# Routing attention with an ELU MLP: three places where the order of work changes

## The chip, the cores and the metric

The kernel runs on one core of a Trainium2 chip. The metric is device time in microseconds (us) of one execution. A core has five engines that run beside each other, each through its own instructions in order: TensorE (PE, whose weight loads are listed apart as PEld), VectorE (DVE), ScalarE (ACT), GpSimd (POOL) and SyncE (SP), which here only issues DMAs.

## The reference

Two parts follow each other. The first is attention in which a query sees only the keys of its own cluster:

```python
q_assign = argmax(einsum('bhsd,hcd->bhsc', q_n, c_n), axis=-1)
k_assign = argmax(einsum('bhsd,hcd->bhsc', k_n, c_n), axis=-1)
mask = q_assign[:, :, :, None] == k_assign[:, :, None, :]
scores = np.where(mask, 0.125 * (q @ k.T), -1e9)
attn = softmax(scores) @ v
```

q, k and v are (4, 8, 768, 64), with 16 clusters per head; the `_n` are normalised vectors. The second is an MLP on the 3072 tokens of width 512: `h = x @ w_in` (512 x 2048), ELU, and `@ w_out` (2048 x 512). Weights arrive as 64-bit floats, and everything is computed in float32.

## The kernel before

**Blocks.** Work is cut into 48 blocks: 4 batches x 3 thirds of the queries (256 each) x 4 pairs of heads. One loop runs over n, the number of the block, and puts out instructions in the order in which they are written; nothing reorders them. In step n stand, one after the other: `values(n - 1)` (p times v into `o_bank`, row sums into a bank `d`, and a short chain on ACT, DVE and POOL, L599 to L607, that makes `xT`), the loads, `scores(n)` (key tile by key tile, L499, with the exponentials L522 on ACT), the masks, and then a part of the MLP of the third that was finished LAG = 7 blocks earlier.

**PSUM.** There are three pairs of banks (`banks`), which scores, hidden layer and row sums take in turn, and the two banks `o_bank` and `f_bank`. A matmul into a bank waits until its former content was read.

**Clusters.** `similar(b, j, at, size)` multiplies queries (j = 0) or keys (j = 1) with the centroids (L377) and transposes the result on DVE (L384). `assign` takes the largest value in each group of 16, compares, and transposes to `hot`, a one-hot matrix (L396 to L410). In batch 0 the mask is added to the scores by another matmul of `hot` (L511), which needs it in the other half of the partitions as well; ACT copies it there (L413), and `masks` (L474) makes the queries' side `qm`. In later batches `key_numbers` (L425, L428) and `query_numbers` (L438, L446) turn `hot` into cluster numbers, and `keep_same` (L457) compares them and zeroes the p of other clusters, in 12 instructions on DVE per block. `sums` adds the tiles of p (L558 to L560), so that the row sums need fewer matmuls.

**The first block.** Before the loop the queries of batch 0 are transposed on PE, the first pair's keys too, `similar(0, 0)` and `assign(0, 0)` are done in two halves, and the other keys are transposed. `scores(0)` then gets the keys' clusters third by third:

```python
for u in range(NT // 2):
    assign(0, 1, u * QS, QS)
    ...
    exponentials(units[u], u)
    weigh(1)
```

**Weights.** `weigh(n)` puts out n of 34 steps that turn a loaded piece of 64-bit weights into float32: on DVE L272, L275, L278 for the piece of two steps ago and L286, L294 for a new one, on ACT L297 between. They are spread over blocks 0 to 8.

**The MLP.** For each third there are four steps: two hidden steps (`hidden`, 32 matmuls of L622, exponential on ACT at L632, POOL at L633), two more, then the products with `w_out` in a scheme with seven instead of eight matrix products (`outer`: four products, then three). The rest of ELU (`elu`, L639 to L643, on DVE) waits in `lag` and comes with the next call of `finish`. The scheme needs sums of blocks of `w_out`: `sum_weights(half)` makes them, four subtractions for each half, on DVE, in block 8 (LAG + 1), one half after the fourth hidden step and one after `finish`.

**The head of a batch.** The clusters of batch b + 1 are found in the last block of batch b. In the first block of the batch (n = 12, 24, 36) come, after `scores(n)`: `key_numbers`, the first `query_numbers`, `keep_same(n)`, `sums(n)`, and then the third hidden step of an earlier third.

Of the kernel before, what the change touches and what calls it, by code (L numbers as in the profile page):

```python
# [15 lines left out]
Alu = mybir.AluOpType  # L16
# [45 lines left out]
def main_path(ctx, tc, c, q, k, v, centroids, moe_w_in, moe_w_out, out):  # L62
    nc = tc.nc
    B, H, S, D = q.shape
# [4 lines left out]
    HS = S // 2  # L69
# [3 lines left out]
    NPR = H // 2  # L73
    KC = DM // P
    FC = DF // P
# [16 lines left out]
    o_bank = long.tile([P, 512], F32, name="o_bank")  # L92
# [77 lines left out]
    for e in range(2):  # L170
# [5 lines left out]
            op=Alu.add,  # L176
# [27 lines left out]
    for e in range(2):  # L204
# [11 lines left out]
        op=Alu.mult,  # L216
# [90 lines left out]
    def weigh(n):  # L307
        for _ in range(n):
            next(rest, None)
# [7 lines left out]
    def w_parts():  # L317
        e_, f_ = w_out[:, : FC // 2, :QS], w_out[:, : FC // 2, QS:]
        g_, h_ = w_out[:, FC // 2 :, :QS], w_out[:, FC // 2 :, QS:]
        return e_, f_, g_, h_  # L320

    def sum_weights(half):

        of = slice(half * FC // 4, (half + 1) * FC // 4)
        e_, f_, g_, h_ = (x[:, of] for x in w_parts())
        t1, t2, t4 = (w_sum[:, n, of] for n in range(3))
        nc.vector.tensor_tensor(t1, f_, e_, op=Alu.subtract)
        nc.vector.tensor_tensor(f_, h_, f_, op=Alu.subtract)
        nc.vector.tensor_tensor(t2, h_, t1, op=Alu.subtract)
        nc.vector.tensor_tensor(t4, g_, t2, op=Alu.subtract)  # L330

# [34 lines left out]

    def similar(b, j, at, size, ps=None):

        if at == 0:
            sim[b, j] = route.tile([P, S], F32, name="sim", tag="sim", bufs=1)
        if ps is None:
            ps = banks()[:, 0]
        cols = slice(at, at + size)
        for pr in range(NPR):
            nc.tensor.matmul(  # L377
                ps[32 * pr : 32 * pr + 32, :size],
                lhsT=cT[:, 32 * pr : 32 * pr + 32],
                rhs=T[b * NPR + pr, j][:, cols],  # L380
                start=True,
                stop=True,
            )
        return lambda: nc.vector.transpose(sim[b, j][:, cols], ps[:, :size])  # L384

    def assign(b, j, at, size):
        if at == 0:
            hot[b, j] = route.tile(
                [P, 2 if b == 0 else 1, S], BF16, name="hot", tag=f"hot{j}", bufs=1
            )  # L390
        cols = slice(at, at + size)
        n = size // NC
        s = sim[b, j][:, cols].rearrange("p (n c) -> p n c", c=NC)
        top = route.tile([P, HS // NC], F32, name="top", tag="top", bufs=1)[:, :n]
        oh = route.tile([P, HS], BF16, name="oh", tag="oh", bufs=1)[:, :size]
        nc.vector.tensor_reduce(top, s, axis=Axis.X, op=Alu.max)  # L396
        at = counted.setdefault(size, [])
        at.append(len(at) + (0 if size == HS else 4 * B - 2))
        at = at[-1]
        nc.vector.scalar_tensor_tensor(  # L400
            oh.rearrange("p (n c) -> p n c", c=NC),
            s,
            1.0,
            top.unsqueeze(2).to_broadcast([P, n, NC]),
            op0=Alu.mult,
            op1=Alu.is_equal,
            accum_out=count[:, at : at + 1],
        )
        h = hot[b, j]
        nc.vector.transpose(h[:, 0, cols], oh)  # L410
        for e in range(2 if b == 0 else 0):
            at = 64 * e
            nc.scalar.copy(h[64 - at : 128 - at, 1, cols], h[at : at + 64, 0, cols])  # L413

    def side(pr, e):
        return int(pr // 2 != e)
# [74 lines left out]
    def scores(n):  # L491
        b, third, pr = blocks[n]
        i = b * NPR + pr
        cols = ts(third, QS)

        def plain(s, kt):
            for e in range(2):
                rows = slice(64 * e, 64 * e + 64)
                nc.tensor.matmul(  # L499
                    s[:, e, ts(kt % 2, QS)],  # L500
                    lhsT=T[i, 1][rows, ts(kt, P)],
                    rhs=T[i, 0][rows, cols],
                    start=n > 0 or kt % 2 == 0,
                    stop=b > 0,
                    skip_group_check=n == 0,
                )

        def mask(s, kt):
            for e in range(2):
                rows = slice(64 * e, 64 * e + 64)  # L510
                nc.tensor.matmul(  # L511
                    s[:, e, ts(kt % 2, QS)],
                    lhsT=hot[b, 1][rows, side(pr, e), ts(kt, P)],
                    rhs=qm[n][rows],
                    start=False,
                    stop=True,
                    skip_group_check=n == 0,
                )

        def exponentials(s, u):  # L520
            p = pu[n, u] = probs.tile([P, 2, 2 * QS], F32, name="p", tag="p")
            nc.scalar.activation(p, s, Act.Exp, scale=SCALE)  # L522

        if n == 0:

            turn_first = similar(0, 1, 0, QS, o_bank)
            turn_rest = similar(0, 1, QS, 2 * QS, f_bank)
            units = [banks() for _ in range(2)]
            for u in range(2):
                for m in range(2):  # L530
                    plain(units[u], 2 * u + m)
            turn_first()
            for u in range(NT // 2):
                assign(0, 1, u * QS, QS)
                if u == 0:
                    turn_rest()
                if u == 1:
                    units.append(banks())
                    for m in range(2):
                        plain(units[2], 4 + m)  # L540
                for m in range(2):
                    mask(units[u], 2 * u + m)
                exponentials(units[u], u)
                weigh(1)
            return
        for u in range(NT // 2):
            s = banks(place["u"][u])
            for m in range(2):
                plain(s, 2 * u + m)
                if b == 0:  # L550
                    mask(s, 2 * u + m)
            exponentials(s, u)
            if n < LAG + 2:
                weigh(1)
# [52 lines left out]
        nc.gpsimd.tensor_tensor(x, x, r, op=Alu.mult)  # L607


    lag = []  # L610

    def finish():
        for step in lag:
# [3 lines left out]
    def hidden(b, third, n):  # L617
        h = banks(place["h"][n % 2])
        hf = h.rearrange("p a (f s) -> p (a f) s", f=2)
        for ch in range(KC):  # L620
            for f in range(4):
                nc.tensor.matmul(  # L622
                    hf[:, f],
                    lhsT=w_in[:, ch, ts(4 * n + f, P)],
                    rhs=xT[b, third][:, ch],
                    start=(ch == 0 and f % 2 == 0),
                    stop=(ch == KC - 1),
                    skip_group_check=True,
                )
        t = g[:, 4 * n : 4 * n + 4]  # L630

        nc.scalar.activation(t, hf, Act.Exp)  # L632
        nc.gpsimd.tensor_scalar(t, t, 1.0, 0.0, op0=Alu.min, op1=Alu.max)  # L633
        finish()
        lag.append(lambda: elu(n, t, hf))
# [147 lines left out]
    for pr in range(NPR):  # L783
        turn(pr, 0)
    turn(0, 1)
    for half in range(2):
        similar(0, 0, half * HS, HS)()
    for pr in range(1, NPR):
        turn(pr, 1)
    for half in range(2):  # L790
        assign(0, 0, half * HS, HS)
    masks(0)

    at_tile = turn_of
    for n in range(len(blocks) + LAG):
# [40 lines left out]
        if n < len(blocks):  # L836
            late = [lambda n=n: sums(n)] if n > LAG else []
            if b > 0:
                third = at // NPR
                q_in = lambda b, third, places: (lambda: query_numbers(b, third, places))  # L840
                if at == 0:
                    key_numbers(b)
                    query_numbers(b, third, [(0, o_bank)])
                    extra[0] = [q_in(b, third, [(1, f_bank), (2, o_bank)])]
                    extra[1] = [q_in(b, third, [(3, f_bank)])]
                elif at % NPR == 0:
                    query_numbers(b, third, [(0, f_bank), (1, o_bank)])
                    extra[0] = [q_in(b, third, [(2, f_bank), (3, o_bank)])]
                keep_same(n)
            if b > 0 and at % NPR == 2:  # L850
                extra[1] = late
            elif not ahead or at + 1 < NB:
                late and late[0]()
# [9 lines left out]
        for m, step in enumerate(main):  # L863
            step()
            for other in extra.get(m, []):
                other()
            if n < LAG + 2 and m < 2:
                weigh(2 if n == LAG else 1)
            if n == LAG + 1 and m > 0:
                weigh(100)  # L870
                sum_weights(m - 1)
        if n == len(blocks) + 1:
            findings()
        if n == len(blocks) + 2:
# [255 lines left out]
```

## Time and profile before

| | |
|---|---|
| median of 9 runs | 1007.83 us (1006.49 to 1009.01) |
| the profiled execution | 1009.9 us, span 1008.1 us |
| PE / PEld busy | 983.6 us (98%) / 770.8 us (76%) |
| DVE / ACT / POOL busy | 661.8 us (66%) / 323.1 us (32%) / 129.6 us (13%) |
| mean granted PE clock | 0.995 of full |

The span reaches from the first instruction to the last. Times in views are us from its start; L499 is line 499 of the kernel before. A view of windows gives, for each stretch, its length, the busy time and the instructions of PE, PEld, DVE, ACT and POOL, the granted clock of PE as a share of full speed, the busy share of the DMA engines, and GB/s. A timeline gives start, duration and instruction, and in brackets how long its engine was idle before it and what ended that.

### The profile page before, as it was taken

The numbers are of one execution on the slowest core, as the hardware profiler recorded it, in microseconds if no ns is written. First come the engines' busy times: TensorE is split into PE (matmuls) and PEld (weight loads), VectorE is DVE, ScalarE is ACT, GpSimd is POOL, SyncE is SP. The second block draws the span as 40 slices with busy tenths as digits, with TensorE's granted clock in tenths as the row PEclk, the third lists the DMA queues.
The fourth block names the chain that finished last, engine by engine and source line by source line (L and its number), as shares of the span: only waits on it lengthen the run. The fifth ranks groups of instructions, "written<-read, shape, count | busy, mean of one in ns | idle before, by whom it ended". The sixth has DMA issues, their size and how long they took to land.

```text
span 1008.1 us, 14617 instructions
## 1 busy us (share of the span) xinstructions
PE 983.6 (98%) x5949; PEld 770.8 (76%) x5949; DVE 661.8 (66%) x1190; ACT 323.1 (32%) x576; POOL 129.6 (13%) x143
## 2 busy tenths in 40 slices
PE   6899999999999999999999999999999999999997
PEld 4566777778878877778788788777877887888886
DVE  7999993666656766796567577587666666663131
ACT  6777432332233232232323232133124224221010
POOL 0001110110210210111111111111021021021010
PEclk9999999999999999999999999999999999999999
DMA  9848132000123123100122113110011010000000
GB/s 288 319 152 200 58 63 53 20 21 25 37 47 63 37 48 64 37 17 17 53 47 48 53 34 61 37 32 16 16 38 32 16 38 26 23 21 1 21 1 24
DMA packets 103962, 55.57 MB, mean 55 GB/s; under 512 B 83408, under 2 KB 96720, under 8 KB 103888
## 3 DMA queue, kind: packets, MB, share of 16 engines
q1 hardware_dynamic: 103888, 54.57, 19.7%
q8 instruction: 48, 0.79, 0.3%
q14 instruction: 26, 0.21, 0.1%
HBM read 48.27 MB, written 6.29 MB: 54 GB/s over the span
## 4 chain that ended last, share of the span: by engine, by line
PE 80%; DVE 17%; ACT 1%; issue 1%; DMA 0%; DVEq 0%; ACTq 0%
PE banks L622 29%; PE f_bank L652 15%; PE o_bank L652 12%; PE o_bank L581 10%; PE banks L499 10%; PE banks L570 2%; DVE ex L272 2%; DVE w_out L275 1%; DVE gT L639 1%; DVE w_out L278 1%; DVE w_in L275 1%; DVE ex L294 1%; DVE w_in L278 1%; DVE oh L400 1%; DVE psum L559 1%
## 5 line engine op out<-in xcount | busy, mean ns | idle before, releaser
L622 PE MATMUL banks<-xT,w_in 128*128 128x256 f32 x1536 | 342.5, 383 | 0.2 <-POOL xT L607 0.2
L622 PEld LDWEIGHTS banks<-xT,w_in 128*128 128x128 f32 x1536 | 290.1, 191 | 48.7 <-issue 9.0
L457 DVE SCALAR_TENSOR_TENSOR p<-qc,kc,p 128x256 f32<-128x256 uint8 x432 | 184.4, 500 | 12.1 <-ACT qc L446 11.9
L499 PE MATMUL banks<-qT,kT 64*128 64x256 f32 x1152 | 146.2, 389 | 2.8 <-DVE gT L639 1.9
L581 PE MATMUL o_bank<-p,v_raw 128*64 128x256 f32 x1152 | 142.9, 385 | 2.2 <-ACT p L522 2.1
L639 DVE SCALAR_TENSOR_TENSOR gT<-gT,banks 128x1024 f32<-128x1024 f32 x48 | 58.4, 1216 | 127.8 <-POOL gT L633 127.8
L632 ACT ACTIVATE gT<-banks 128x1024 f32<-128x1024 f32 x48 | 49.1, 1023 | 286.0 <-PE banks L622 286.0
L522 ACT ACTIVATE p<-banks 128x1024 f32<-128x1024 f32 x144 | 139.3, 1036 | 1.2 <-PE banks L511 0.7
L499 PEld LDWEIGHTS banks<-qT,kT 64*128 64x128 f32 x1152 | 101.4, 186 | 40.5 <-issue 17.8
L581 PEld LDWEIGHTS o_bank<-p,v_raw 128*64 128x64 f32 x1152 | 78.3, 137 | 55.5 <-issue 14.5
L633 POOL TENSOR_SCALAR gT<-gT 128x1024 f32<-128x1024 f32 x48 | 53.6, 1117 | 333.4 <-ACT gT L632 333.4
L607 POOL TENSOR_TENSOR xT<-xT,r 128x256 f32<-128x256 f32 x48 | 40.7, 848 | 427.9 <-DVE r L604 377.7
L599 ACT ACTIVATE r<-banks 128x256 f32<-128x256 f32 x48 | 18.4, 383 | 240.8 <-PE banks L570 240.8
L652 PE MATMUL o_bank<-w_out,gT 128*128 128x256 f32 x416 | 95.1, 382 | 0.0
L652 PEld LDWEIGHTS o_bank<-w_out,gT 128*128 128x128 f32 x416 | 78.2, 190 | 13.5 <-issue 3.3
L652 PE MATMUL f_bank<-w_out,gT 128*128 128x256 f32 x352 | 79.6, 379 | 0.0
L603 DVE TENSOR_TENSOR e<-e,r 128x256 f32<-128x256 f32 x48 | 20.3, 422 | 85.3 <-ACT r L602 85.3
L652 PEld LDWEIGHTS f_bank<-w_out,gT 128*128 128x128 f32 x352 | 66.9, 190 | 9.1
L559 DVE TENSOR_TENSOR psum<-psum,p 128x1024 f32<-128x1024 f32 x40 | 52.7, 1317 | 1.6
L652 PE MATMUL f_bank<-w_sum,gT 128*128 128x256 f32 x224 | 50.9, 380 | 1.0 <-DVE o_sb L692 1.0
L558 DVE TENSOR_TENSOR psum<-p 128x1024 f32<-128x1024 f32 x40 | 48.8, 1221 | 0.0
L652 PEld LDWEIGHTS f_bank<-w_sum,gT 128*128 128x128 f32 x224 | 42.3, 190 | 7.8 <-DVE o_sb L692 2.2
(134 smaller groups left out, 820.9 us busy)
## 6 DMA issues: line engine op xcount, KB each, us to landing
v_raw<-in_v_dram SPq DMA_DIRECT2D x48, 384.0 KB, 3.2
w_sum<-in_moe_w_out_dram SPq DMA_DIRECT2D x12, 512.0 KB, 5.1
out_dram<-o_sb SPq DMA_DIRECT2D x24, 256.0 KB, 2.0
q_raw<-in_q_dram SPq DMA_DIRECT2D x48, 96.0 KB, 3.2
k_raw<-in_k_dram SPq DMA_DIRECT2D x48, 96.0 KB, 3.1
w_sum<-in_moe_w_in_dram SPq DMA_DIRECT2D x8, 512.0 KB, 8.3
w_out<-in_moe_w_in_dram SPq DMA_DIRECT2D x8, 512.0 KB, 11.1
w_out<-in_moe_w_out_dram SPq DMA_DIRECT2D x4, 512.0 KB, 3.7
```

Of the source, the lines that this page charges most:

```text
L457: nc.vector.scalar_tensor_tensor(p, qc[b, third][:, 2 * pr + e], kc[b][:, 2 * u + m, 2 * pr + e : 2 * pr + e + 1], p, op0=Alu.is_equal, op ...
L499: nc.tensor.matmul(s[:, e, ts(kt % 2, QS)], lhsT=T[i, 1][rows, ts(kt, P)], rhs=T[i, 0][rows, cols], start=n > 0 or kt % 2 == 0, stop=b > 0 ...
L522: nc.scalar.activation(p, s, Act.Exp, scale=SCALE)
L558: nc.vector.tensor_tensor(to, pu[n, 0], pu[n, 1], op=Alu.add)
L559: nc.vector.tensor_tensor(to, to, pu[n, 2], op=Alu.add)
L581: nc.tensor.matmul(o_bank[64 * e : 64 * e + 64, :QS], lhsT=raw["v", n][:, e, kt], rhs=p[:, e, ts(m, QS)], start=(kt == 0), stop=(kt == NT ...
L607: nc.gpsimd.tensor_tensor(x, x, r, op=Alu.mult)
L622: nc.tensor.matmul(hf[:, f], lhsT=w_in[:, ch, ts(4 * n + f, P)], rhs=xT[b, third][:, ch], start=(ch == 0 and f % 2 == 0), stop=(ch == KC - 1),
L632: nc.scalar.activation(t, hf, Act.Exp)
L633: nc.gpsimd.tensor_scalar(t, t, 1.0, 0.0, op0=Alu.min, op1=Alu.max)
L639: nc.vector.scalar_tensor_tensor(t, t, -1.0, hf, op0=Alu.add, op1=Alu.max)
L652: nc.tensor.matmul(to[:, :QS], lhsT=left[:, f], rhs=right[:, f], start=(f == 0), stop=(f == FC // 2 - 1),)
```

## The change

There are three parts.

1. At the head of a batch, `key_numbers`, the first `query_numbers`, `keep_same` and `sums` are put into a list `between`, which `hidden` works off after the second of its four rounds of matmuls.
2. `sum_weights` becomes a generator: the first two subtractions of a half stand ahead of the last ELU step of that third, those of the other half and the remaining four after it. `sums` of block 9 (LAG + 2) moves behind the second product.
3. Before the first block, only the first half of the queries' clusters is found, and kept in the memory of `g_sum`. The second half's similarity is put out after the second unit of scores, its transpose and `assign` after the third. `assign` copies only one way; the other way is copied for all columns at once in `other_rows`. The first three weight steps come after all that.

```diff
+    def sum_weights():
+
+        halves = [slice(half * FC // 4, (half + 1) * FC // 4) for half in range(2)]
+        for of in halves:
...
+            nc.vector.tensor_tensor(t1, f_, e_, op=Alu.subtract)
+            nc.vector.tensor_tensor(f_, h_, f_, op=Alu.subtract)
+            yield
+        for of in halves:
...
+            nc.vector.tensor_tensor(t2, h_, t1, op=Alu.subtract)
+            nc.vector.tensor_tensor(t4, g_, t2, op=Alu.subtract)
+        yield
...
     def similar(b, j, at, size, ps=None):
 
-        if at == 0:
+        if (b, j) == (0, 0):
+            sim[b, j] = g_sum.rearrange("p f n -> p (f n)")[:, :S]
+        elif at == 0:
             sim[b, j] = route.tile([P, S], F32, name="sim", tag="sim", bufs=1)
...
         nc.vector.transpose(h[:, 0, cols], oh)
-        for e in range(2 if b == 0 else 0):
-            at = 64 * e
-            nc.scalar.copy(h[64 - at : 128 - at, 1, cols], h[at : at + 64, 0, cols])
+        if b == 0:
+            nc.scalar.copy(h[64:, 1, cols], h[:64, 0, cols])
+
+    def other_rows(j):
+
+        nc.scalar.copy(hot[0, j][:64, 1], hot[0, j][64:, 0])
...
                 exponentials(units[u], u)
-                weigh(1)
+                if u == 1:
+                    turn_more = similar(0, 0, HS, HS, f_bank)
+            turn_more()
+            assign(0, 0, HS, HS)
+            for j in range(2):
+                other_rows(j)
+            weigh(3)
             return
...
                     stop=(ch == KC - 1),
                     skip_group_check=True,
                 )
+            if ch == 1:
+                for other in between:
+                    other()
+                between.clear()
...
-    for half in range(2):
-        similar(0, 0, half * HS, HS)()
+    similar(0, 0, 0, HS)()
     for pr in range(1, NPR):
         turn(pr, 1)
-    for half in range(2):
-        assign(0, 0, half * HS, HS)
+    assign(0, 0, 0, HS)
     masks(0)
...
                 if at == 0:
-                    key_numbers(b)
-                    query_numbers(b, third, [(0, o_bank)])
+
+                    between.append(lambda b=b: key_numbers(b))
+                    between.append(q_in(b, third, [(0, o_bank)]))
+                    between.append(lambda n=n: keep_same(n))
+                    between.extend(late)
+                    late = []
...
-            if b > 0 and at % NPR == 2:
+            if b > 0 and at % NPR == 2 or n == LAG + 2:
                 extra[1] = late
...
-            if n == LAG + 1 and m > 0:
+            if n == LAG + 1 and m == 1:
                 weigh(100)
-                sum_weights(m - 1)
+                sums_left = sum_weights()
+                next(sums_left)
+        if n == LAG + 1:
+            for _ in sums_left:
+                pass
```

More of the change, by code (lines that the diff above doesn't have):

```diff
@@ L320, in w_parts @@
         return e_, f_, g_, h_
[L322 to L330, printed above, removed]
+    def sum_weights():
+        halves = [slice(half * FC // 4, (half + 1) * FC // 4) for half in range(2)]
+        for of in halves:
+            e_, f_, g_, h_ = (x[:, of] for x in w_parts())
+            t1, t2, t4 = (w_sum[:, n, of] for n in range(3))
+            nc.vector.tensor_tensor(t1, f_, e_, op=Alu.subtract)
+            nc.vector.tensor_tensor(f_, h_, f_, op=Alu.subtract)
+            yield
+        for of in halves:
+            e_, f_, g_, h_ = (x[:, of] for x in w_parts())
+            t1, t2, t4 = (w_sum[:, n, of] for n in range(3))
+            nc.vector.tensor_tensor(t2, h_, t1, op=Alu.subtract)
+            nc.vector.tensor_tensor(t4, g_, t2, op=Alu.subtract)
+        yield
     T, sim, hot, qm, qc, kc = {}, {}, {}, {}, {}, {}
@@ L607, in values @@
         nc.gpsimd.tensor_tensor(x, x, r, op=Alu.mult)
-    lag = []
+    lag, between = [], []
     def finish():
@@ L841, in main_path @@
                 if at == 0:
-                    key_numbers(b)
-                    query_numbers(b, third, [(0, o_bank)])
+                    between.append(lambda b=b: key_numbers(b))
[3 more added lines that the diff above has]
+                    late = []
                     extra[0] = [q_in(b, third, [(1, f_bank), (2, o_bank)])]
                     extra[1] = [q_in(b, third, [(3, f_bank)])]
[L846 to L849, printed above, removed]
-            if b > 0 and at % NPR == 2:
+                else:
+                    if at % NPR == 0:
+                        query_numbers(b, third, [(0, f_bank), (1, o_bank)])
+                        extra[0] = [q_in(b, third, [(2, f_bank), (3, o_bank)])]
+                    keep_same(n)
+            if b > 0 and at % NPR == 2 or n == LAG + 2:
                 extra[1] = late
```

## The prediction

> **What bounds the kernel now.** I read the page first, then the windows by stage, then the timeline where PE or DVE stands idle. PE is busy 983.6 us of the span of 1008.1, so all gaps of PE together are 24.5 us; 5.3 of them lie before the first matmul and 6.1 after the last, and the change touches neither. What it can win is in the gaps between, and in stretches at a lower clock. The windows (span, then busy us of PE, PEld, DVE, ACT, POOL, then clock):
>
> ```profile
> 14.40:46.80 32.40, 27.37 (x220) 16.56 (x220) 29.73 (x67) 24.38 (x44) 1.03 (x1) 0.95 0.98 372
> 46.80:145.00 98.20, 95.26 (x737) 67.44 (x734) 96.27 (x163) 62.06 (x104) 11.86 (x11) 1.00 0.46 119
> 160.00:200.00 40.00, 40.00 (x268) 29.93 (x264) 20.57 (x34) 11.21 (x19) 4.95 (x6) 1.00 0.10 34
> 200.00:220.00 20.00, 18.37 (x95) 14.65 (x94) 15.44 (x30) 6.84 (x13) 1.76 (x2) 0.91 0.07 21
> 220.00:1000.00 780.00, 778.23 (x4504) 623.42 (x4504) 482.06 (x856) 210.15 (x383) 107.41 (x99) 1.00 0.13 33
> ```
>
> From 160 us on PE is the bound, with holes at the heads of batches. From 14 to 145 us DVE is full (96.27 of 98.20): it rebuilds the weights (steps of L272 to L294) beside everything else, and PE follows it. How DVE's order holds PE in the start is seen in the timeline (start, us, instruction, then in brackets the idle time before it and who ended it):
>
> ```profile
> 18.81 0.41 DVE L384 STREAM_TRANSPOSE sim<-o_bank 128x256 f32<-128x256 f32 x1
> 26.03 0.69 DVE L272 SCALAR_TENSOR_TENSOR ex<-w_sum,ex 128x512 uint32<-128x512 uint32 x1 [0.98 <-ACT ex L297]
> 34.05 0.72 ACT L297 ACTIVATE ex<-ex,off 128x512 uint32<-128x512 uint32 x1 [1.88 <-DVE ex L294]
> 35.45 0.70 PE L499 MATMUL banks<-qT,kT 64*128 64x256 f32 x4 [0.88 <-ACT e L600]
> 38.17 0.99 PE L581 MATMUL o_bank<-p,v_raw 128*64 128x256 f32 x4 [1.36 <-ACT p L522]
> 46.72 0.43 DVE L603 TENSOR_TENSOR e<-e,r 128x256 f32<-128x256 f32 x1 [0.97 <-ACT r L602]
> ```
>
> ACT stands at L297 until DVE gives it the exponents of a weight step; L599 to L602 and the next exponentials queue behind it, and PE waits for those. After 14.4 us DVE itself idles only twice, 0.98 and 0.97 us. The other places that the change touches, on PE:
>
> ```profile
> 139.70 0.70 PE L499 MATMUL banks<-qT,kT 64*128 64x256 f32 x4 [1.42 <-DVE gT L639]
> 152.40 3.72 PE L652 MATMUL f_bank<-w_sum,gT 128*128 128x256 f32 x16 [0.79 <-DVE o_sb L692]
> 204.94 0.23 PE L425 MATMUL f_bank<-index,hot 128*128 128x8 bf16 x3 [1.42 <-DVE hot L410]
> 205.41 8.86 PE L622 MATMUL banks<-xT,w_in 128*128 128x256 f32 x32
> 444.18 0.23 PE L425 MATMUL f_bank<-index,hot 128*128 128x8 bf16 x3 [0.77 <-DVE hot L410]
> 681.53 0.23 PE L425 MATMUL f_bank<-index,hot 128*128 128x8 bf16 x3 [0.78 <-DVE hot L410]
> ```
>
> The same 32 matmuls of L622 take 7.17 us elsewhere. Why they took 8.86 here is in the windows of 1 us (the clock is the third number from the end):
>
> ```profile
> 205.00:206.00 1.00, 1.00 (x7) 0.68 (x8) 0.62 (x3) 0.68 (x2) 0.20 (x1) 0.80 0.00 0
> 206.00:207.00 1.00, 1.00 (x4) 0.81 (x3) 0.86 (x2) 0.11 (x1) 0.53 (x1) 0.50 0.03 8
> 209.00:210.00 1.00, 1.00 (x6) 0.88 (x5) 1.00 (x4) 0.00 (x0) 0.00 (x0) 0.99 0.00 0
> ```
>
> The clock was 0.50 for about 3.4 us after the gap, and PE lost 1.7 us. The waits at 35.45 and 38.17 were followed by the same (0.50 from 38.4 to 41.8); the equal wait at 139.70 was not.
>
> **Heads of batches.** key_numbers, the first query_numbers, keep_same and sums move behind the first 16 matmuls of the first MLP step (half of 7.1 us, so 3.55). The keys' last one-hot is there at 204.9, and PE now comes to it at 203.1 + 3.55 = 206.7: no wait. Removed are 0.21 + 1.42, 0.77 and 0.78, together 3.2 us. The 0.7 us of small matmuls stay. In the profiled execution the clock's 1.7 us go too, since PE now has no gap there.
>
> What the move delays is DVE: qc lands at about 208.1 instead of 206.1, the 12 mask multiplies (5.02) end at 213.1 and the sums (1.22 + 1.23 + 0.69) at 216.2. Queued behind them is L639 of the third hidden step, which ran at 216.49 and now runs at 216.2. PE needs the masked p first in values, after a second hidden step, at 218.9, and the sums 2.7 us later. Cover: 5 us. Without it each head would give back 2 to 3 us. On ACT L428 and the first cast go ahead of L632, which only comes after the hidden step.
>
> **Weights' sums.** Before, all eight subtractions in two groups of four stand in DVE's queue; the first group (132.93 to 138.43) holds L639 of the last hidden step, and PE waits 1.42 us for its bank. After, two of them (1.22 + 1.94) stand ahead: L639 starts at 136.05 and ends at 137.3, while PE asks at 138.3. So 1.42 goes. The other six follow and end at about 145, as now. sums of block 9 (3.15 us, from 147.64) now come after the second product instead of before the first, so L687 and L692 are done at 148.9 and 149.3; PE, now 1.42 earlier, asks for f_bank at 150.1. So 0.79 goes as well. Late next is nothing: row sums of block 9 are at 156, their input at 153.6. Sum: -2.2.
>
> **Start.** It takes 8 matmul passes, one transpose (0.5) and one assign (1.65) of DVE, six copies of ACT (three of 0.51, three of 0.41) and two weight steps (0.63 each) from ahead of, or between, the first masks, and puts them behind the third. What stays in front is bounded elsewhere. kT's last copy on ACT waits for its six PE transposes, which wait for the last k load: issued at 11.8, 4.4 on its way, so 16.2; the copy ends at 18.04, and the first key similarity is ready at 18.75 against 18.81 now. PE's own 16 score passes of L499 end at 21.5 either way.
>
> - PE: masks of unit 0 end at 21.7 (22.3 now), exponentials at 21.8, 23.7, 25.6 (22.30, 24.23, 26.91), values(0) at 25.4 instead of 26.80. PE leads by 1.4 us.
> - DVE: it idles from 16.7 (queries' half done) to 18.75, 2.05 us, where it now does the second half. After the keys it waits 0.6 us for the second half's matmuls, which stand behind unit 1's masks on PE; transpose and assign end at 26.6, two weight steps at 27.9. L272 needs L297, and on ACT that now stands behind the exponentials (to 26.6), one copy of 0.51 and the two of other_rows. Those are 64x768; from the 64x384 (0.51) and 64x256 (0.41) copies I estimate 0.83 each. L297 ends at 29.6, so DVE idles 1.7. Sum 2.05 + 0.6 + 1.7 - 0.98 = 3.4, with 0.2 of lost overlap at the restarts 3.6 us late.
> - DVE is full from here to 145, so this isn't made up, and PE's lead of 1.4 turns into a longer wait at the place of 35.45. One thing gives: the 0.97 us at 46.72, which came from the slow clock. If the clock is back by 41.8, it goes wholly; if the longer wait of PE (about 6 us, 33 to 39) holds it down one stretch more, 0.8 returns. I take +0.4.
>
> Start in the profiled execution: 3.6 - 0.97 + 0.4 = +3.0. Bounds: 2.65 and 4.4; -1.4 if DVE's delay met slack that I can't see.
>
> [...]
>
> **Sum.** Profiled execution: +3.0 - 2.2 - 3.2 - 1.7 = -4.1 against its own time of 1009.9 (span 1008.1 and 1.8 around it), 1005.8. It is 2.1 above the median of 1007.83. The nine runs spread over 2.5 us, and the two clock losses are worth 1.7 + 0.97; I take it that the median has about half of them. Then the heads' clock gives 0.85 and the start costs 3.6 - 0.5 + 0.4 = 3.5: 3.5 - 2.2 - 3.2 - 0.85 = -2.75, so 1005.1 (-0.27%). With start and clock at their bounds, 1003.4 to 1006.8. A measurement of this kernel can tell about 0.2%, 2.0 us, from no change, so this is close to that line.
>
> **Rivals.**
> - Slower: the clock at the start. PE's wait from 33 to 39 is four times that of any now; if the clock stays at 0.50 over three stretches of 3.4 us, PE loses 5.1, with only some 0.3 us of idle time in each block of 9.2 to take it up: 3.6 + 5.1 - 5.4 = +3.3, 1011.1. It decides from 3.6 us of half clock on (3.6 + 1.8 = 5.4). For it: the stretch from 38.4 holds only some 2 us of PE work. Against it: both stretches now end after one. 0.11.
> - No clock loss in the median run, and the start's whole 3.6 + 0.4: 4.0 - 5.4 = -1.4, 1006.4. For it: the median is 2.1 under the profiled run. 0.22.
> - Two groups of sums do as before: the wait at 139.70 returns at f_bank, where the cover is only 0.8 us: 2.2 lost, 1007.3. 0.05.
> - The start costs nothing, or keeps PE's 1.4: -5.4 - 0.85 = 1001.6, or 1000.2. For it: PE's gaps from 23 to 27 do shrink. Against it: DVE's 96.27 of 98.20. 0.10.
> - The forecast: 0.52.
>
> **How the numbers follow.** Faster by over 0.2%: 0.52 + 0.10 = 0.62; within: 0.22 + 0.05 = 0.27; slower: 0.11. The range goes from the last rival's near end, 1001.6, to past the third's 1007.3, 1007.5; left out are the slower case and half of the last, 0.16.
>
> **What would show it.** Right: no PE wait before L425, and 7.1 us of L622 with 0.7 between its halves; L639 ahead of the last six subtractions, no wait at L499 and f_bank; DVE's first L272 at about 29.6 and still full to 145; a PE wait of some 6 us before scores of block 1. Wrong: a first L272 before 27, first key transpose well before 18.7, DVE gaps after 50 us, or a half clock of over 4 us at 40.

## The result and the profile after

The changed kernel takes 1004.25 us in the median of 9 runs (1003.17 to 1005.11), the kernel before 1007.73 (29 runs, 1005.92 to 1009.01): a ratio of 0.9966, 95% interval 0.9958 to 0.9974, so 3.5 us less. The profiled execution takes 1003.53 us, span 1001.8. Lines of the new kernel that answer to those of before: L385 for L377 and L392 for L384 (similarity and its transpose), L510 for L499 (scores), L598 for L581 (values), L639 for L622 (hidden), L660 for L639 (ELU), L673 for L652 (product), L436 for L425 (key numbers), L533 for L522 (exponentials), L424 is `other_rows`, L617, L619, L620 are L600, L602, L603. Windows of the changed kernel, columns as before:

```profile
14.40:46.80 32.40, 24.95 (x205) 14.44 (x203) 27.77 (x62) 22.24 (x35) 1.03 (x1) 0.89 0.95 354
46.80:145.00 98.20, 96.62 (x753) 69.10 (x752) 96.27 (x166) 63.42 (x109) 11.86 (x11) 1.00 0.49 123
200.00:220.00 20.00, 20.00 (x120) 15.77 (x120) 15.44 (x30) 7.55 (x12) 4.50 (x3) 1.00 0.06 19
```

In the first, the start, PE and DVE are both about 2 us less busy than before (27.37 and 29.73), and the clock is 0.89. In the second PE is busy 1.4 us longer, in the third 1.6, the gap at the head; it is full there. DVE's queue in the start (timeline of DVE, instructions with idle time before them), then ACT's beside it:

```profile
17.80 0.45 DVE L392 STREAM_TRANSPOSE sim<-o_bank 128x256 f32<-128x256 f32 x1 [1.71 <-PE o_bank L385]
23.55 0.58 DVE L392 STREAM_TRANSPOSE g_sum<-f_bank 128x384 f32<-128x384 f32 x1 [0.65 <-PE f_bank L385]
28.84 0.69 DVE L272 SCALAR_TENSOR_TENSOR ex<-w_sum,ex 128x512 uint32<-128x512 uint32 x1 [1.58 <-ACT ex L297]
```

```profile
26.50 1.56 ACT L424 COPY hot<-hot 64x768 bf16<-64x768 bf16 x2
28.08 1.33 ACT L297 ACTIVATE ex<-ex,off 128x512 uint32<-128x512 uint32 x2
```

These are the three waits that the prediction listed (2.05, 0.6, 1.7), the last because L297 stands behind the two copies. PE in the timeline, at the start, at the sums, and at the first and second head:

```profile
38.18 1.23 PE L510 MATMUL banks<-qT,kT 64*128 64x256 f32 x4 [5.69 <-ACT e L617]
40.89 1.12 PE L598 MATMUL o_bank<-p,v_raw 128*64 128x256 f32 x4 [0.21 <-ACT p L533]
...
137.52 0.70 PE L510 MATMUL banks<-qT,kT 64*128 64x256 f32 x4
...
140.98 3.72 PE L673 MATMUL o_bank<-w_out,gT 128*128 128x256 f32 x16
...
151.45 3.62 PE L673 MATMUL f_bank<-w_sum,gT 128*128 128x256 f32 x16
...
201.94 3.72 PE L639 MATMUL banks<-xT,w_in 128*128 128x256 f32 x16
205.50 0.29 PE L436 MATMUL f_bank<-index,hot 128*128 128x8 bf16 x6
205.73 0.39 PE L449 MATMUL o_bank<-hot,index 32*128 32x256 bf16 x2
206.04 3.72 PE L639 MATMUL banks<-xT,w_in 128*128 128x256 f32 x16
...
442.01 0.29 PE L436 MATMUL f_bank<-index,hot 128*128 128x8 bf16 x6
```

No line from 137.52 on has a bracket: the waits of 1.42, 0.79, 1.42 and 0.77 are gone, and none has come in their place. The clock, in windows of 1 us:

```profile
36.00:37.00 1.00, 0.00 (x0) 0.00 (x0) 1.00 (x4) 0.23 (x1) 0.00 (x0) 0.50 1.02 397
41.00:42.00 1.00, 1.00 (x6) 0.62 (x8) 0.97 (x2) 1.00 (x2) 0.32 (x1) 0.50 0.96 347
206.00:207.00 1.00, 1.00 (x6) 0.87 (x5) 0.23 (x1) 0.61 (x2) 0.00 (x0) 1.00 0.00 0
```

PE waits 5.69 us, from 32.5 to 38.18. The clock falls to 0.50 inside this wait, at 35.4, and comes back at 42.2, after 6.8 us, twice the 3.4 of either stretch in the trace of before; 2.8 of these 6.8 us lie in the wait and slow nothing. At the head the clock stays full.

Where the profiled execution's time went can be read off at marks that both traces have. Each row is the move of a mark from before to after, less the move of the mark ahead of it:

| mark | before, after (us) | its part | predicted |
|---|---|---|---|
| first transpose of the queries' similarity (L384, L392) | 14.36, 13.71 | -0.65 | 0 |
| first hidden step of the first third | 95.14, 96.82 | start: +2.33 | +3.0 |
| values behind the fourth product | 156.05, 154.99 | sums: -2.74 | -2.2 |
| values behind head 1 | 221.95, 217.44 | -3.45 (1.7 of it clock) | -1.63 - 1.7 |
| values behind head 2 | 459.51, 453.96 | -1.04 | -0.77 |
| values behind head 3 | 696.86, 690.48 | -0.83 | -0.78 |
| sum | | -6.38 | -4.1 |

The first row isn't the change's: over all kernels of this study that mark lies anywhere from 13.7 to 14.4, whichever start they have. The row of head 2 holds one more wait of PE than the prediction listed, in the trace of before:

```profile
393.90 3.72 PE L652 MATMUL f_bank<-w_sum,gT 128*128 128x256 f32 x16 [0.21 <-DVE o_sb L692]
```

The changed kernel's trace has no such wait.

### The profile page after: what moved, and what is told of

It is laid out like the page before. It is cut to its first block, busy times and chain, and to the rows that moved or that the text cites. A ratio compares the mean times of both kernels' runs of the same rounds, so it can differ in the third digit from the quotient of the medians.

```text
span 1001.8 us, 14614 instructions
## 1 busy us (share of the span) xinstructions
PE 979.9 (98%) x5949; PEld 768.5 (77%) x5949; DVE 663.4 (66%) x1190; ACT 322.4 (32%) x573; POOL 133.9 (13%) x143
## 4 chain that ended last, share of the span: by engine, by line
PE 88%; DVE 9%; SPq 1%; ACT 0%; DMA 0%; issue 0%; DVEq 0%
PE banks L639 32%; PE f_bank L673 16%; PE o_bank L673 13%; PE banks L510 11%; PE o_bank L598 11%; DVE ex L272 2%; PE banks L587 2%; DVE w_in L275 1%; DVE w_in L278 1%; DVE w_out L275 1%; DVE ex L294 1%; DVE w_out L278 1%; PE banks L385 1%; SPq L135 1%; PE f_bank L449 1%; DVE w_out L286 1%
## 5 line engine op out<-in xcount | busy, mean ns | idle before, releaser
L639 PE MATMUL banks<-xT,w_in 128*128 128x256 f32 x1536 | 341.6, 382 | 0.3 <-POOL xT L624 0.3
L639 PEld LDWEIGHTS banks<-xT,w_in 128*128 128x128 f32 x1536 | 288.7, 190 | 49.0 <-issue 10.7
L510 PE MATMUL banks<-qT,kT 64*128 64x256 f32 x1152 | 147.2, 390 | 6.2 <-ACT e L617 5.7
L598 PE MATMUL o_bank<-p,v_raw 128*64 128x256 f32 x1152 | 142.5, 385 | 1.1 <-ACT p L533 1.1
L533 ACT ACTIVATE p<-banks 128x1024 f32<-128x1024 f32 x144 | 139.2, 1036 | 2.0 <-PE banks L522 1.7
L510 PEld LDWEIGHTS banks<-qT,kT 64*128 64x128 f32 x1152 | 101.7, 187 | 44.0 <-issue 18.3
L660 DVE SCALAR_TENSOR_TENSOR gT<-gT,banks 128x1024 f32<-128x1024 f32 x48 | 58.4, 1216 | 114.4 <-POOL gT L654 114.4
L598 PEld LDWEIGHTS o_bank<-p,v_raw 128*64 128x64 f32 x1152 | 78.1, 137 | 54.3 <-issue 14.2
L654 POOL TENSOR_SCALAR gT<-gT 128x1024 f32<-128x1024 f32 x48 | 57.9, 1206 | 324.0 <-ACT gT L653 324.0
L673 PE MATMUL o_bank<-w_out,gT 128*128 128x256 f32 x416 | 95.1, 382 | 0.0
L673 PEld LDWEIGHTS o_bank<-w_out,gT 128*128 128x128 f32 x416 | 78.2, 190 | 13.5 <-issue 3.3
L673 PE MATMUL f_bank<-w_out,gT 128*128 128x256 f32 x352 | 79.6, 379 | 0.0
L620 DVE TENSOR_TENSOR e<-e,r 128x256 f32<-128x256 f32 x48 | 20.3, 422 | 84.3 <-ACT r L619 84.3
L673 PEld LDWEIGHTS f_bank<-w_out,gT 128*128 128x128 f32 x352 | 66.9, 190 | 9.1
L576 DVE TENSOR_TENSOR psum<-psum,p 128x1024 f32<-128x1024 f32 x40 | 54.8, 1370 | 1.5
L673 PE MATMUL f_bank<-w_sum,gT 128*128 128x256 f32 x224 | 50.8, 380 | 0.0
L673 PEld LDWEIGHTS f_bank<-w_sum,gT 128*128 128x128 f32 x224 | 42.4, 190 | 6.5 <-DVE o_sb L713 0.8
```

Of the source, the lines that this page charges most:

```text
L510: nc.tensor.matmul(s[:, e, ts(kt % 2, QS)], lhsT=T[i, 1][rows, ts(kt, P)], rhs=T[i, 0][rows, cols], start=n > 0 or kt % 2 == 0, stop=b > 0 ...
L576: nc.vector.tensor_tensor(to, to, pu[n, 2], op=Alu.add)
L598: nc.tensor.matmul(o_bank[64 * e : 64 * e + 64, :QS], lhsT=raw["v", n][:, e, kt], rhs=p[:, e, ts(m, QS)], start=(kt == 0), stop=(kt == NT ...
L639: nc.tensor.matmul(hf[:, f], lhsT=w_in[:, ch, ts(4 * n + f, P)], rhs=xT[b, third][:, ch], start=(ch == 0 and f % 2 == 0), stop=(ch == KC - 1),
L660: nc.vector.scalar_tensor_tensor(t, t, -1.0, hf, op0=Alu.add, op1=Alu.max)
L673: nc.tensor.matmul(to[:, :QS], lhsT=left[:, f], rhs=right[:, f], start=(f == 0), stop=(f == FC // 2 - 1),)
```

## The experiments

**The theory.** The three parts are independent: heads and sums take PE gaps away, and the start costs what it adds to DVE's idle time, because DVE is full up to 145 us. **The rivals.** The start costs through the clock and not through DVE; or ACT's copies and the weight steps cost it and not the queries; or the cover of DVE at the heads is smaller than I took it. The kernels of the experiments have line numbers of their own, so a line is known by its operands.

### Each part alone, and two together

*heads_only*: the kernel before, with part 1 of the change and nothing else.

```diff
                 if at == 0:
-                    key_numbers(b)
-                    query_numbers(b, third, [(0, o_bank)])
+                    between.append(lambda b=b: key_numbers(b))
+                    between.append(q_in(b, third, [(0, o_bank)]))
+                    between.append(lambda n=n: keep_same(n))
...
```

> The kernel before with the first part alone (numbers of a new batch's clusters behind the first half of its first MLP step). Theory: the three gaps of PE ahead of the key numbers go, 1.7, 1.0 and 1.0 us by the shift of the later groups in the two traces, and the half clock after the first of them where a run had it (1.7): -3.7 to -5.4 us, about 1003.2. Rival: the mask multiplies, 2 to 3 us later on VectorE, give it back: -1 us or less, with a wait of PE at the values of that block.

Measured: 1003.09 us, ratio 0.9960 (0.9947 to 0.9973), 4.7 us less.

*sums_only*: the kernel before, with part 2 alone.

```diff
-                sum_weights(m - 1)
+                sums_left = sum_weights()
+                next(sums_left)
+        if n == LAG + 1:
+            for _ in sums_left:
+                pass
```

> The kernel before with the second part alone (subtractions of the weights split around the last ELU, sums of block 9 after the second product). Theory: the waits at 139.7 and 152.4 go, 1.42 + 0.79 us as listed and some 0.5 more by the shift of the later groups: -2.2 to -2.8 us, about 1005.2. Rival: the wait moves on to the fourth product or to the row sums of block 9: within 0.5 us of the kernel before.

Measured: 1004.99 us, ratio 0.9975 (0.9966 to 0.9984), 2.8 us less. Its trace keeps the wait at the head, but not what followed it in the trace of before. PE's timeline and a window of 1 us:

```profile
200.53 0.23 PE L431 MATMUL f_bank<-index,hot 128*128 128x8 bf16 x3 [1.42 <-DVE hot L416]
```

```profile
202.00:203.00 1.00, 1.00 (x6) 0.90 (x5) 1.00 (x3) 0.00 (x0) 0.12 (x1) 1.00 0.02 8
```

The same 1.42 us, and the clock stays at 1.00. So the gap alone doesn't bring the clock's loss at the head; what does was not shown.

*start_only*: the kernel before, with part 3 alone.

```diff
-    for half in range(2):
-        similar(0, 0, half * HS, HS)()
+    similar(0, 0, 0, HS)()
...
-                weigh(1)
+                if u == 1:
+                    turn_more = similar(0, 0, HS, HS, f_bank)
+            turn_more()
+            assign(0, 0, HS, HS)
...
+            weigh(3)
```

> The kernel before with the third part alone (first block given half of the queries' clusters and one copied half of the rows). Theory: VectorE, full from 14 to 145 us, loses about 3.4 us in three waits (2.05, 0.6, 1.6 against 0.98 before) and only 0.97 comes back at the place of 46.7: +2.5 to +3.6 us, about 1010.7, and a wait of PE of over 5 us before the scores of block 1. Rival: PE's lead of 1.4 us at the first values lasts, or the delay of VectorE is absorbed: -1.4 to 0 us.

Measured: 1010.29 us, ratio 1.0029 (1.0018 to 1.0041), 2.5 us more. DVE's three waits are there again (1.50, 0.65 and 1.58). The three parts alone add up to 5.0 us less, the whole change has 3.5. Each of these figures is known to about 1 us either way, so the runs neither show that the parts share something nor that they are quite independent.

*heads_sums*: the changed kernel with part 3 undone, which is the kernel before with parts 1 and 2 (the diff of start_only, backwards).

> The changed kernel with its third part undone (first and second part on the kernel before). Theory: the sum of the first two, -5.9 to -8.2 us, about 1000.7, so some 3 us below the changed kernel's 1004.25. Rival that the start costs nothing or gains: 1004.3 or above. Third reading, that the parts share gaps: less than the sum of the runs with one part each.

Measured: 1000.70 us (999.60 to 1000.99), ratio 0.9931 (0.9918 to 0.9945), 7.1 us less; the sum of the two alone is 7.5. It beats both kernels, and of the versions below only rows_only is level with it: the start takes back half of what the other two parts bring. DVE's idle time from the first transpose of the queries' similarity to 145 us, in its timeline:

```profile
25.47 0.69 DVE L272 SCALAR_TENSOR_TENSOR ex<-w_sum,ex 128x512 uint32<-128x512 uint32 x1 [0.99 <-ACT ex L297]
28.36 0.69 DVE L272 SCALAR_TENSOR_TENSOR ex<-w_sum,ex 128x512 uint32<-128x512 uint32 x1 [0.20 <-ACT ex L297]
```

1.19 us, where the changed kernel has 3.94.

### What in the start costs: copies, weight steps, clock

*after_again*: the changed kernel once more.

> The changed kernel itself, on the chip and in the rounds of the three others: 1003.2 to 1005.1, median about 1004.2.

Measured: 1004.02 us, ratio 0.9960 (0.9946 to 0.9973). In this trace the half clock lies from 38.2 to 45, 2.8 us later than in the first, and DVE waits once more:

```profile
50.00 0.43 DVE L620 TENSOR_TENSOR e<-e,r 128x256 f32<-128x256 f32 x1 [1.05 <-ACT r L619]
```

ACT's r comes from the row sums of values(1), which PE does up to 48 us.

*rows_late*: `other_rows` behind the three weight steps.

```diff
-            for j in range(2):
-                other_rows(j)
             weigh(3)
+            for j in range(2):
+                other_rows(j)
```

> The changed kernel with the two copies of other_rows put behind the first three weight steps instead of ahead of them. Theory: VectorE's wait of 1.58 us at its first L272 is for L297, which stands behind the copies on ScalarE (1.56 us); with them behind it, VectorE waits 0.3 us at most, and since it is full to 145 us the whole kernel is 1.2 to 1.6 us shorter: about 1002.8. Rival: the wait is made by the exponentials and the late second half, or VectorE's delay isn't what the end sees: within 0.4 us of the changed kernel (1004.25).

Measured: 1003.41 us, ratio 0.9953 (0.9940 to 0.9967): 0.6 us under after_again, where I expected 1.2 to 1.6; the two intervals overlap almost wholly, so the medians alone show no gain. DVE's timeline:

```profile
27.62 0.69 DVE L272 SCALAR_TENSOR_TENSOR ex<-w_sum,ex 128x512 uint32<-128x512 uint32 x1 [0.18 <-ACT ex L297]
48.45 0.42 DVE L620 TENSOR_TENSOR e<-e,r 128x256 f32<-128x256 f32 x1 [1.19 <-ACT r L619]
```

The wait at L272 did fall from 1.58 to 0.18, as the theory has it. The trace of after_again has a wait at L620 too (1.05), so against it DVE idles 1.3 us less in all (3.72 against 5.05, table below). The first trace of the changed kernel has none at L620, and against that one (3.94) nearly all of the gain is lost again.

*steps_between*: a weight step after each unit again, as in the kernel before.

```diff
+                weigh(1)
             turn_more()
...
-            weigh(3)
```

> The changed kernel with one weight step after each unit of the first block again, as before the change, instead of three at the end. Theory: two of VectorE's three waits (0.65 for the second half's matmuls, 1.58 at L272) are filled, only the one for the keys (1.7) stays: -1.8 to -2.3 us against the changed kernel, about 1002.2, although the first values begin 1 us or more later on PE. Rival, that PE's early start counts: +0.6 to +1.3 us, about 1005.2.

Measured: 1005.04 us, ratio 0.9972 (0.9959 to 0.9984): 1.0 us over after_again, where I expected about 2 less. My expectation fell. DVE's timeline, then ACT's:

```profile
34.18 0.69 DVE L272 SCALAR_TENSOR_TENSOR ex<-w_sum,ex 128x512 uint32<-128x512 uint32 x1 [1.56 <-ACT ex L297]
50.20 0.42 DVE L620 TENSOR_TENSOR e<-e,r 128x256 f32<-128x256 f32 x1 [1.59 <-ACT r L619]
```

```profile
30.61 1.56 ACT L424 COPY hot<-hot 64x768 bf16<-64x768 bf16 x2
32.18 1.22 ACT L485 ACTIVATE qm<-hot,minus,big 64x256 bf16<-64x256 bf16 x2
33.43 1.33 ACT L297 ACTIVATE ex<-ex,off 128x512 uint32<-128x512 uint32 x2
```

With the steps spread, the copies and L485 come later and stand ahead of another L297. The wait has moved, from 28.84 to 34.18, and kept its size.

*clock_kept*: 24 matmuls more inside PE's wait before the scores of block 1, their results unused.

```diff
+            for _ in range(24 if (n, u) == (1, 2) else 0):
+                nc.tensor.matmul(
+                    f_bank[:, :QS], lhsT=ident, rhs=T[0, 0][:, :QS], start=True, stop=True
+                )
```

> The changed kernel with 24 added matmuls into f_bank, whose result nobody reads, in PE's wait of 5.7 us before the third unit of block 1's scores. Theory: the half clock from 35.4 to 42.2 goes, but costs next to nothing, since PE waits for VectorE and ScalarE there: within 0.4 us of the changed kernel. Rival, the slow clock at the start as a price of its own: -0.8 to -1.7 us.

Measured: 1006.05 us, ratio 0.9983 (0.9974 to 0.9992), 2.0 us over after_again. It didn't do what I meant: PE's timeline has

```profile
32.78 10.63 PE L566 MATMUL f_bank<-qT,ident 128*128 128x256 f32 x48
```

48 records, two for each fp32 matmul, 0.22 us each. PE came to the scores at 43.34 instead of 38.66. The clock stayed at 1.00, but nothing follows from that for its price. What it does tell: PE being 4.7 us late, with the clock full, cost 2.0.

*clock_short*: the same with 10 matmuls.

> The changed kernel with 10 matmuls more (20 passes, about 4.4 us at full clock) into a free bank, inside PE's wait of 5.7 us before the scores of block 1; their results are not used. They should end at about 37.4, before the scores' 38.2. The clock should be 1.00 from 33 to 46 us. Theory (half clock during the first values of block 1 makes ACT's r late, and DVE idles 1 us at L620): that idle time goes, 0.7 to 1.2 us under the changed kernel (about 1003.0). Rival (PE's half clock costs nothing there, since DVE is full anyway, and the idle time at L620 has another cause): within 0.4 us of the changed kernel, and a wait at L620 stays.

Measured: 1003.62 us, ratio 0.9960 (0.9946 to 0.9973), the same ratio as after_again. PE's timeline:

```profile
32.74 4.58 PE L566 MATMUL f_bank<-qT,ident 128*128 128x256 f32 x20
38.50 0.70 PE L510 MATMUL banks<-qT,kT 64*128 64x256 f32 x4 [1.18 <-ACT e L621]
```

This time they fit, the clock is 1.00 from 33 to 46 us, and DVE has no wait at L620. The median moved by 0.4 us, which the measurement can't tell from nothing. So the half clock goes with 1.05 us of DVE's idle time at L620 in one execution (that of after_again) and with none in another (the first trace of the changed kernel, where it ends at 42.2 and L620 doesn't wait); in the median no price of it is seen. The intervals, some 1.3 us either way, don't shut out a small one. But the trace without half clock has the same interval as the first of the changed kernel (83.18 and 83.11 us, table below), so the rival that makes the clock the cause of the start's 3 to 3.5 us falls.

### Which part of the start

*rows_only*: parts 1 and 2, and of part 3 only the copies (one way in `assign`, `other_rows` behind the third masks).

```diff
-        for e in range(2 if b == 0 else 0):
-            at = 64 * e
-            nc.scalar.copy(h[64 - at : 128 - at, 1, cols], h[at : at + 64, 0, cols])
+        if b == 0:
+            nc.scalar.copy(h[64:, 1, cols], h[:64, 0, cols])
...
                 weigh(1)
+            for j in range(2):
+                other_rows(j)
```

> Parts 1 and 2, and of part 3 only the rows: the first block's three early copies of ACT into the other half of hot are left for two larger ones behind its third masks; queries and weight steps as before. Theory (DVE's idle time up to 52 us is what the start costs): DVE's order is untouched, ACT has about 1.3 us less ahead of its first L297, so the wait of 0.99 us at DVE's first L272 shrinks and none of 1.5 us comes in its place; 0.3 to 1.0 us under the kernel with parts 1 and 2 (ratio about 0.9925 to the kernel before). Rival (the two larger copies, 1.56 us on ACT, hold a later L297 as they did in the changed kernel): a wait of 1 to 1.6 us at another L272, 0.5 to 1.5 us over it (ratio about 0.9940).

Measured: 1000.86 us, ratio 0.9931 (0.9917 to 0.9945), the same as heads_sums. Neither forecast came true: DVE's timeline shows both at once,

```profile
25.65 0.69 DVE L272 SCALAR_TENSOR_TENSOR ex<-w_sum,ex 128x512 uint32<-128x512 uint32 x1 [0.66 <-ACT ex L297]
31.76 0.69 DVE L272 SCALAR_TENSOR_TENSOR ex<-w_sum,ex 128x512 uint32<-128x512 uint32 x1 [0.82 <-ACT ex L297]
```

a shorter first wait (0.99 before) and a new one of 0.82 behind the larger copies, 1.48 against 1.19 in all.

*q_only*: parts 1 and 2, and of part 3 only the queries' second half.

```diff
-    for half in range(2):
-        similar(0, 0, half * HS, HS)()
+    similar(0, 0, 0, HS)()
...
+                if u == 1:
+                    turn_more = similar(0, 0, HS, HS, f_bank)
                 weigh(1)
+            turn_more()
+            assign(0, 0, HS, HS)
```

> Parts 1 and 2, and of part 3 only the queries: the second half of the first block's queries is compared and assigned behind its third masks; copies and weight steps as before. Theory: DVE waits about 2.0 us for the keys at 16 to 18 us and 0.6 us for the half moved, and nothing takes the 2 us back, while L297 has no larger copies ahead of it: 2.0 to 2.8 us over the kernel with parts 1 and 2, so about 4.5 us under the kernel before (ratio 0.9955), and with the rows' part this is the whole of the start. Rival (the start's cost is the weight steps and copies around L297, the queries' wait is made up): under 1 us over it (ratio 0.9935).

Measured: 1004.06 us, ratio 0.9965 (0.9952 to 0.9979). That is 3.4 us over heads_sums (0.9965 - 0.9931), more than the 2.0 to 2.8 that I expected, and level with the whole change: the queries' half alone has the start's cost. DVE's timeline:

```profile
18.19 0.45 DVE L392 STREAM_TRANSPOSE sim<-o_bank 128x256 f32<-128x256 f32 x1 [1.50 <-PE o_bank L385]
25.28 0.69 DVE L272 SCALAR_TENSOR_TENSOR ex<-w_sum,ex 128x512 uint32<-128x512 uint32 x1 [0.80 <-ACT ex L297]
33.34 0.69 DVE L272 SCALAR_TENSOR_TENSOR ex<-w_sum,ex 128x512 uint32<-128x512 uint32 x1 [0.51 <-ACT ex L297]
49.38 0.42 DVE L615 TENSOR_TENSOR e<-e,r 128x256 f32<-128x256 f32 x1 [1.61 <-ACT r L614]
```

DVE stands 1.50 us waiting for keys that can't come earlier. The moved half then delays the steps behind it, and with them ACT's L297 and e; PE gets e late (a wait of 2.96 before the scores) and r comes late to DVE (1.61).

**All starts in one table.** Each trace is measured from its first transpose of the queries' similarity to the first hidden step of the first third; DVE's idle time in between (the brackets of its timeline) is taken off. The last column is the median of the runs; all these kernels but the first have parts 1 and 2.

| kernel | interval (us) | DVE idle | rest | median |
|---|---|---|---|---|
| before | 80.78 | 1.95 | 78.83 | 1007.73 |
| heads_sums | 80.00 | 1.19 | 78.81 | 1000.70 |
| rows_only | 80.27 | 1.48 | 78.79 | 1000.86 |
| rows_late | 82.98 | 3.72 | 79.26 | 1003.41 |
| changed kernel | 83.11 | 3.94 | 79.17 | 1004.25 |
| clock_short | 83.18 | 3.99 | 79.19 | 1003.62 |
| q_only | 83.54 | 4.42 | 79.12 | 1004.06 |
| after_again | 84.29 | 5.05 | 79.24 | 1004.02 |
| steps_between | 84.88 | 5.78 | 79.10 | 1005.04 |
| clock_kept | 85.96 | 6.70 | 79.26 | 1006.05 |

The rest is 78.8 with the old order and 79.1 to 79.3 with the queries' half moved; what the 0.3 to 0.5 more are was not shown. So the interval is DVE's work plus what DVE idles, whoever caused it: DVE bounds the start. And the kernel is late by it: against heads_sums the profiled executions from rows_only down to clock_kept are 0.3, 3.2, 2.8, 3.2, 3.4, 4.2, 4.4 and 5.4 us longer, their intervals 0.3, 3.0, 3.1, 3.2, 3.5, 4.3, 4.9 and 6.0.

### The cover at the heads

*between_late*: heads_sums, with the batch's numbers behind all 32 matmuls of the hidden step.

```diff
-            if ch == 1:
+            if ch == 3:
                 for other in between:
```

> The kernel with parts 1 and 2, with the batch's numbers put behind all 32 matmuls of the first hidden step instead of the first 16, so 3.55 us later. Theory (cover of about 5 us on DVE, of which the change used some 2): masked p about 1.5 us and sums about 1 us before PE asks for them, no PE gap at the heads, within 0.7 us of the kernel with parts 1 and 2 (ratio 0.9931). Rival (the cover was already used up): a PE wait of 2 to 3 us at values or row sums of the batch's first block at each of the three heads, 6 to 9 us in all (ratio about 1.0005).

Measured: 1001.48 us, ratio 0.9940 (0.9927 to 0.9954), 0.8 over heads_sums (not clear of the intervals), so near the theory's 0.7 and far from the rival's 6 to 9. PE's timeline at head 1, then DVE's:

```profile
206.93 0.26 PE L444 MATMUL o_bank<-hot,index 32*128 32x256 bf16 x1 [0.44 <-ACT qc L452]
...
217.29 0.60 PE L576 MATMUL banks<-psum,ones 128*64 128x256 f32 x4
```

```profile
214.96 0.69 DVE L566 TENSOR_TENSOR psum<-psum 128x512 f32<-128x512 f32 x1
```

The sums end at 215.65, 1.6 us before PE's row sums, which don't wait. With the 3.55 us of the further move that makes a cover of about 5 us where the change put them. The trace's new gaps are the 0.44 us at qc, once at each head, and one of 0.22 at 386.61 that the kernel before has too (393.90) and heads_sums hasn't: 1.5 us in all against the 0.8 measured.

## Why the prediction was right, point by point

- **Heads.** Right. Listed: 3.18 us of gaps; measured at the marks 1.75 + 1.04 + 0.83 = 3.62 without the clock, and 0.21 of this is the wait at 393.90, which the list left out. The mask multiplies start 4.8 us after the hidden step (predicted 5.0), the sums end at 215.4, 4.6 before PE's row sums at 220.08 (predicted cover 5). DVE in the changed kernel, at the sums of the weights and at head 1:

```profile
137.73 1.21 DVE L660 SCALAR_TENSOR_TENSOR gT<-gT,banks 128x1024 f32<-128x1024 f32 x1
206.77 4.84 DVE L468 SCALAR_TENSOR_TENSOR p<-qc,kc,p 128x256 f32<-128x256 uint8 x12 [2.18 <-ACT qc L457]
214.75 0.69 DVE L577 TENSOR_TENSOR psum<-psum 128x512 f32<-128x512 f32 x1
```

- **Sums.** Right in place: L660 starts at 137.73, which is the predicted 136.05 plus the 1.68 that all is late there. Mis-sized: 2.74 against 2.2. The term was taken from the idle figures in brackets, and these leave something out: 16 matmuls last 3.72 us, 32 last 7.17, so 16 more take 3.45, from which I estimate that a group's end is booked 0.27 us after the point at which the next could have followed. Two gaps here make 0.54, which is the difference. It is no rule for every gap: head 1 gave 0.12 more than its two brackets, head 3 0.05 more than its one, and of the 0.27 at head 2 the wait at 393.90 is 0.21.
- **Start.** Right in mechanism and size. DVE's waits 1.71, 0.65, 1.58 against 2.05, 0.6, 1.7; the first L272 is 15.13 us behind the first transpose of the queries' similarity, before 11.67, so 3.46 late against 3.6. The 0.2 of lost overlap in the 3.6 was my estimate, and no run shows such a loss; what the table of the starts shows is a rest 0.3 to 0.5 us longer where the queries' half moved. PE's wait is 5.69 against about 6. The wait of 0.97 at 46.72 went, as said; the 0.4 that I let return is 0 in one trace and 1.05 in the other. In the median the part costs 2.5 us alone (1.8 to 4.1 by its interval) and 3 to 3.5 on top of the others, where I took 3.5. Of the signs against me one came in full: half clock of over 4 us at 40, here 6.8, from 35.4 to 42.2. It was no sign of a high price, since 2.8 of it lay in PE's wait and DVE bounds this stretch. Another came in part: the first key transpose is at 17.80 and not at 18.7, of which 0.65 is the earlier first mark. What I did not see is that the queries' half alone has the whole cost; the copies, which made the wait of 1.58, are free when the queries stay in front (rows_only 1000.86 us, heads_sums 1000.70).
- **Clock.** The row at 204.94 was no rule: sums_only and start_only have the same gap of 1.42 and no half clock behind it in their traces. The mean clock of the single runs of the kernel before hints at how often it comes: 32 of 44 have 0.994 or 0.995 and a median of 1008.0, 12 have 0.997 and a median of 1006.5. This reads as one loss more, worth 1.5 us, in three runs of four, where I had the median at about half of the losses. Only one of these runs has a trace, and the mean also counts half clock behind the last matmul (3.8 us in that trace), so which loss it is stays open. At the start both traces of the changed kernel have 6.8 us of half clock: in after_again it begins at 38.2, 5.2 us into PE's wait, in the first at 35.4, 2.9 us into it. Beside it DVE idled 1.05 us at L620 in the one and not at all in the other.
- **Sum.** Predicted 1005.1, measured 1004.25. In the profiled execution the sum was -4.1 and is -6.4. The 2.3 between are the first mark's 0.65 (the chance of one execution), 0.67 of the start (3.0 against 2.33), 0.54 of the sums and 0.44 of the heads. The last two may be of every execution (one trace of each kernel shows them), and together they are of the size of the 0.85 by which the median was missed; the share of executions with a clock loss works on the same side. The slower rival (half clock over three stretches, dear from 3.6 us on) had two stretches, 6.8 us, and they cost little; the rival in which the start is free needed DVE to have slack, and the table shows none.

## What to carry to other kernels

Before work is moved behind something more urgent, ask what the engine does in the time set free: here DVE had nothing else to do until the keys came, so the half that was done early was free, and doing it late cost 3.4 us. On an engine that is full up to a known mark, add up the brackets from a common start to that mark: the sum is the price of an order of work, whichever wait it takes the form of (here 1.19 us in an interval of 80.00, 6.70 in one of 85.96). A wait that is cut at one place of such a queue counts only if the next one (here r at L620, 1.19 us in rows_late, or another L297, 1.56 in steps_between) doesn't take it back.

## What the hardware showed that I had not expected

- The stretches of half clock between matmuls are 3.413 and 3.413 us long in the trace of before and 6.827, twice that, in the first of the changed kernel. The granted clock changes at 38.34, 41.76, 205.60, 209.01 and, behind the last matmul, 1004.32 in the one, and at 35.38, 42.21 and, behind the last matmul, 997.94 in the other. From the end of the first stretch of before to the start of the second are 163.84 us, 48 times 3.413.
- The same gap was followed by half clock in one trace and not in two others. Ahead of head 1 PE idles 0.21 + 1.42 us in all three. In the trace of before the gap ends at 204.94, and the clock is at 0.50 from 205.60 to 209.01; in those of sums_only (to 200.53) and start_only (to 207.14) it is 1.00 in every window of 1 us from 180 to 230. The 1.42 us before 139.70 in the trace of before weren't followed by half clock either. What decides was not shown.
- The idle time in brackets can be short of what a gap costs: at the two gaps of the sums by about 0.27 us each (an estimate, from 3.72 us for 16 matmuls and 7.17 for 32, and the 2.74 measured there against 2.2), at the heads by less (0.12 at head 1, 0.05 at head 3).
